# Attention with a feed-forward layer: one-bank PSUM tiles, 129-column products with v, and two jobs moved from VectorE to ScalarE

## The chip, the cores and the metric

The kernel runs on one core of a Trainium2 chip. Its time is the device time of one execution in microseconds (us); the median of several executions counts, and lower is better. Five engines work side by side: TensorE (PE in the profile; its weight loads are PEld), VectorE (DVE), ScalarE (ACT), GpSimd (POOL) and SyncE (SP), which issues the DMAs. Matrix products land in PSUM, which has eight banks of 512 float32 columns; all eight are in use here.

## The reference

```python
def _attn_ref(q, k, v):            # 8 batches, 8 heads, 1152 positions, 64 wide
    q_pool = q.reshape(B, H, S // 2, 2, D).mean(axis=3)
    scores = np.matmul(q_pool, k.transpose(0, 1, 3, 2)) / np.sqrt(D)
    scores = scores - np.max(scores, axis=-1, keepdims=True)
    attn = np.exp(scores)
    attn = attn / (np.sum(attn, axis=-1, keepdims=True) + 1e-09)
    return np.matmul(attn, v).astype(np.float32)

def _moe_ref(x, w_in, w_out):      # x: 4608 x 512, w_in: 512 x 2048, w_out: 2048 x 512
    h = x @ w_in
    g = h * np.cos(h)
    return (g @ w_out).astype(np.float32)

def reference(**kwargs):
    attn_out = _attn_ref(q, k, v)
    x = attn_out.transpose(0, 2, 1, 3).reshape(B * S, H * D)
    return _moe_ref(x, w_in, w_out)
```

## The kernel before, in words

The 64 heads are worked on two at a time: 32 pairs, each in ten units. Nine units of a pair hold the 128 keys of one block for both heads and 512 pooled queries each (2 x 512 score columns); one unit, the rest, holds the 64 remaining queries of each head against all nine key blocks (1024 and 128 columns). A unit runs as follows.

- `s_unit` writes the scores into a PSUM tile `st` of two banks (four products of 512 columns; a second product per bank subtracts the row maximum, which was folded into the operands beforehand). There is one such tile.
- `soft` (L1281 on) takes the exponential of all 1024 columns in one ScalarE instruction (L1299), casts the result to float16 (L1305), and forms the low half, the exponential minus its float16 copy: on GpSimd in two pieces of 512 columns (L1311), or, in every third unit from unit 80 on, on VectorE in one piece (L1307). `DSH` is that three.
- `av` (L1332 on) multiplies the 128 x 128 blocks of the exponential (loaded as weights) with v. v is 64 wide with a column of ones beside it, which gives the row sums. In float16 there are three products for each query tile of 128: high half with v's high half and the ones (65 columns), high half with v's low half (64 columns), low half with v's high half (65 columns). They add up in two PSUM banks, `ava` for the first head (and the rest) and `avb` for the second. For pairs 0 to 3, and for part of the key blocks of pairs 4 and 5, float32 products of 65 columns stand in their place (`NF32`).
- `av_end` (L1415 on) divides by the row sums on VectorE into `xp`.

The row maxima of a later pair come from products of their own, in PSUM tiles `mx` (printed as `m` or `mx`) of two banks, one tile at a time: `mx_main` (L788), `mx_rest` (L813), `mx_mixed` (L835), `mx_mixed_rest` (L851) and the `head_` and `first_` forms for the first three pairs. VectorE reduces 1024 columns at once (L811). Also ahead of a pair, q is pooled and cast twice over into `q1s` (`prep_q1`: one cast of 1024 columns and two of 64 x 128), on ScalarE for the first `QACT` = 6 pairs (L744) and on VectorE after (L746), and v's bound is taken (`v_max_begin`: the sum of squares on ScalarE for the first `VACT` = 6 pairs, L1115, the largest absolute value on VectorE after, L1119).

The feed-forward layer runs in 18 chunks of 256 tokens between the units: `ffn1` (L1586) into PSUM tiles `f` (two of one bank), two ScalarE passes and one VectorE pass out of them (L1610, L1613, L1614), a sine (L1518), a product on VectorE (L1524), a cast on ScalarE (L1535) and a subtraction on GpSimd (L1536), then `ffn2` (L1646). After the last pair only such chunks are left.

The order on each engine is written out by `arrange`. It takes all instructions in the order of the code, finds who needs whom (whole PSUM banks count), gives each a cost (`estimate`, with `HAND` for the hand-over between engines), and lays them out one after another: the next on an engine is the one that is ready by these costs and stands first in the code, moved by the `SHIFT` table. The engines then run their queues in that fixed order.

## Time and profile before

| | |
|---|---|
| median of 3 runs | 1517.22 us (1516.85 to 2447.02; the highest stands alone) |
| profiled execution | 1520.95 us, of which the trace spans 1519.2 us |
| PE busy | 1489.5 us (98%) |
| ACT busy | 1175.4 us (77%) |
| DVE busy | 1105.9 us (73%) |
| POOL busy | 922.4 us (61%) |
| mean granted clock of TensorE | 0.996 of full speed |

Busy time of an engine is the union of its instructions in the trace. Matmuls are pipelined, so the duration printed for one of them is longer than the time from its start to the next one's start; what a matmul takes of the engine is read from starts. A wait is idle time in front of an instruction, put down to whoever released it last.

### The profile page before, as it was taken

Reading aid. Unit: us, or ns where it says so; the run is one execution under the profiler, and the core shown is the slowest. Engines: PE = TensorE matmul, PEld = TensorE weight load, DVE = VectorE, ACT = ScalarE, POOL = GpSimd, SP = SyncE. Lnnn points to the kernel's source line nnn. Section 1 sums busy time; section 2 is a strip of 40 time slices with the busy share of each in tenths; the row PEclk is TensorE's granted clock in tenths of the full one; section 3 lists DMA queues with packets and bytes.
Section 4 is the critical chain, followed back from the end, with each engine's and each line's share of the span. In section 5 each row is a group of like instructions: output and inputs, shape, how many; then the busy total and the mean of one; then the engine's idle time right before and its main releaser. Section 6 shows DMA issues by size and latency. Waiting matters only on the chain.

```text
span 1519.2 us, 39331 instructions
## 1 busy us (share of the span) xinstructions
PE 1489.5 (98%) x16774; PEld 1027.7 (68%) x16774; DVE 1105.9 (73%) x1556; ACT 1175.4 (77%) x1475; POOL 922.4 (61%) x806
## 2 busy tenths in 40 slices
PE   6999999999999999999999999999999999999998
PEld 4777787657666576666667657666766667766665
DVE  7889987777878687887757877978788876442332
ACT  4867779888988789887967887997888888954442
POOL 4645757795775858577555576676766675430222
PEclk9999999999999999999999999999999999999999
DMA  9989543534255353435432335335344332001000
GB/s 268 246 237 188 151 109 69 107 82 119 73 108 97 89 110 80 110 91 114 85 75 64 80 74 125 76 91 126 82 104 99 73 63 32 10 27 30 20 16 22
DMA packets 226111, 145.15 MB, mean 96 GB/s; under 512 B 202448, under 2 KB 204752, under 8 KB 223888
## 3 DMA queue, kind: packets, MB, share of 16 engines
q1 hardware_dynamic: 225936, 142.65, 40.8%
q8 instruction: 131, 2.15, 0.6%
q14 instruction: 44, 0.36, 0.1%
HBM read 74.45 MB, written 10.49 MB: 56 GB/s over the span
## 4 chain that ended last, share of the span: by engine, by line
PE 89%; DVE 4%; DMA 3%; ACT 2%; issue 1%; SPq 0%; POOL 0%; ACTq 0%; DVEq 0%; POOLq 0%
PE f L1586 21%; PE f L1646 19%; PE st L1249 15%; PE ava L1325 8%; PE avb L1325 6%; PE m L797 6%; PE st L1272 2%; PE avb L1374 2%; PE mx L1646 1%; DMA wraw<-in_moe_w_in_dram 1%; PE mx L840 1%; PE st L1586 1%; PE mx L819 1%; DVE mxs L811 1%; DMA k<-kst 1%
## 5 line engine op out<-in xcount | busy, mean ns | idle before, releaser
L1311 POOL TENSOR_TENSOR pp<-e,pp 128x512 f16<-128x512 f32 x374 | 456.0, 1240 | 288.6 <-ACT pp L1305 151.3
L1586 PEld LDWEIGHTS <-w 128*128 128x128 f16 x3456 | 331.6, 98 | 61.5 <-issue 0.8
L1586 PE MATMUL f<-xT,w 128*128 128x256 f16 x3048 | 366.3, 273 | 0.0
L811 DVE TENSOR_REDUCE mxs<-m 128x2 f32<-128x1024 f32 x232 | 283.1, 1220 | 94.6 <-PE m L797 93.9
L1299 ACT ACTIVATE e<-st 128x1024 f32<-128x1024 f32 x267 | 272.5, 1021 | 96.5 <-PE st L1249 79.7
L1646 PE MATMUL f<-w,g 128*128 128x512 f16 x1440 | 333.7, 379 | 0.1
L1305 ACT CAST pp<-e 128x1024 f16<-128x1024 f32 x267 | 279.1, 1045 | 14.8 <-PE avb L1325 3.7
L1536 POOL TENSOR_TENSOR g<-hsc,g 128x512 f16<-128x512 f32 x144 | 192.1, 1354 | 157.7 <-ACT g L1535 150.3
L1325 PEld LDWEIGHTS <-pp 128*128 128x128 f16 (+1 forms) x7062 | 237.9, 100 | 65.5 <-issue 11.3
L1646 PEld LDWEIGHTS <-g 128*128 128x128 f16 x1680 | 158.5, 98 | 175.1 <-issue 0.7
L1249 PE MATMUL st<-q1T,k 128*128 128x512 f16 x576 | 219.3, 381 | 2.7 <-ACT pp L1299 1.9
L1249 PE MATMUL st<-q2T,k 128*128 128x512 f16 x576 | 219.2, 381 | 0.0
L1325 PE MATMUL ava<-vc,pp 128*128 128x65 f16 (+5 forms) x4502 | 218.2, 199 | 0.0
L1325 PE MATMUL avb<-vc,pp 128*128 128x65 f16 (+1 forms) x3052 | 179.0, 197 | 0.0
L1249 PEld LDWEIGHTS <-k 128*128 128x128 f16 x1152 | 104.5, 99 | 100.0 <-issue 11.0
L1524 DVE TENSOR_TENSOR hsc<-hsc,y 128x512 f32<-128x512 f32 x144 | 129.3, 933 | 37.8 <-ACT y L1518 37.5
L1614 DVE SCALAR_TENSOR_TENSOR y<-f,r1a,y 128x512 f32<-128x512 f32 x127 | 94.7, 746 | 66.6 <-ACT y L1613 64.1
L797 PE MATMUL m<-k,q1T 128*128 128x512 f16 x464 | 138.4, 380 | 4.2 <-ACT es L1299 1.7
L1307 DVE TENSOR_TENSOR pp<-e,pp 128x1024 f16<-128x1024 f32 x80 | 118.7, 1484 | 23.0 <-ACT pp L1305 22.7
L1610 ACT ACTIVATE hsc<-f,small 128x512 f32<-128x512 f32 x127 | 86.7, 682 | 58.4 <-PE f L1586 57.7
L1535 ACT CAST g<-hsc 128x512 f16<-128x512 f32 x144 | 83.4, 613 | 27.5 <-PE f L1646 26.2
L728 POOL TENSOR_TENSOR kst<-kld,kst 128x1152 f16<-128x1152 f32 x30 | 73.2, 2441 | 30.9 <-ACT kst L727 30.7
(189 smaller groups left out, 1852.0 us busy)
## 6 DMA issues: line engine op xcount, KB each, us to landing
vld<-in_v_dram SPq DMA_DIRECT2D x32, 576.0 KB, 4.5
kld<-in_k_dram SPq DMA_DIRECT2D x30, 576.0 KB, 4.2
qld<-in_q_dram SPq DMA_DIRECT2D x30, 576.0 KB, 4.4
k<-k SPq DMA_DIRECT2D x31, 288.0 KB, 3.7
wraw<-in_moe_w_in_dram SPq DMA_DIRECT2D x8, 1024.0 KB, 8.4
wraw<-in_moe_w_out_dram SPq DMA_DIRECT2D x8, 1024.0 KB, 6.1
out_dram<-ob SPq DMA_DIRECT2D x32, 256.0 KB, 2.5
left<-lx SPq DMA_DIRECT2D x64, 16.0 KB, 1.8
```

Of the source, the lines that this page charges most:

```text
L797: nc.tensor.matmul(banks[h], q1T[n][:, h * QT + t, :], kmain(n, k1[n % 3], c, h), start=True, stop=True, skip_group_check=True,),
L811: nc.vector.reduce_max(mxs[n][:, t : t + QT + 1 : QT, c], m, axis=AX.X)
L1249: nc.tensor.matmul(s[:, y, :].rearrange("p (t c) -> p t c", c=P), kcol(p, w, j, h), x[:, h * QT : (h + 1) * QT, :], start=part == 0, stop= ...
L1299: nc.scalar.activation(e, s, AF.Exp, scale=exp_scale, bias=l_add)
L1305: nc.scalar.copy(pp[:, 0, c0:n], e[:, c0:n])
L1307: nc.vector.tensor_sub(pp[:, 1, c0:n], e[:, c0:n], pp[:, 0, c0:n])
L1311: nc.gpsimd.tensor_sub(pp[:, 1, c], e[:, c], pp[:, 0, c])
L1325: mm = nc.tensor.matmul(out, w, x, start=start, stop=False, skip_group_check=True)
L1524: nc.vector.tensor_mul(hj, hj, y[:, j : j + 2])
L1536: nc.gpsimd.tensor_sub(gt[:, 1], hj, gt[:, 0])
L1586: mm = nc.tensor.matmul(ps[:, fi, :], w1[wt][:, hp, fs], ck.xT[hp][:, xi, cs], start=n == 0, stop=n == 3 * HP - 1, skip_group_check=True,)
L1646: nc.tensor.matmul(po, gt[:, gi, f % 2, ts_], w2[wt][:, f, :], start=f == 0 and (gi, wt) == (0, 0), stop=f == NF - 1 and (gi, wt) == (1, 0),)
```

## The change

- The PSUM tiles `st` and `mx` of two banks become one-bank tiles, two of each. A unit's scores stand in two tiles, and the exponential takes one instruction of 512 columns for each; the casts after it stay whole. The row maxima are reduced bank by bank. Tiles for the rests of the maxima take one bank where two were taken.
- In float16 units, three of four query tiles of the second head and two of four of the first take the high half's two products as one of 129 columns, written over v's low and high halves side by side. The two sums then lie 64 columns apart in PSUM (`COL`), and `av_end` adds them: it takes the row sums in two strided pieces for the first head, multiplies in two pieces, and adds the low part of each of the five tiles with one VectorE instruction (L1469 of the changed kernel).
- `QACT` and `VACT` go from 6 to 32: all casts of `q1s` and all bounds of v run on ScalarE.
- `DSH` goes from 3 to 5: from unit 80 on, every fifth low half is formed on VectorE instead of every third.
- `arrange` gets other costs: new constants in `estimate`, a hand-over of 0.203 us from PE, 0 from SP and 0.035 us from the others (0.21, 0.08 for ACT, 0.06 before), `INTO` added on the receiving engine, `OVER` subtracted where an instruction starts before the one ahead of it has ended, and a reader of a PSUM bank now waits for all writes to that bank. `SHIFT` holds the same numbers in another form.

```diff
-DSH = 3
+DSH = 5
...
-QACT = 6
+QACT = 32
...
-VACT = 6
+VACT = 32
...
-    "e": NE, "big": NBIG, "pp": NPP, "q1T": 3, "q2T": 2, "xp": NXP, "xT": NXT, "g": NG, "f": 2,
+    "e": NE, "big": NBIG, "pp": NPP, "q1T": 3, "q2T": 2, "xp": NXP, "xT": NXT, "g": NG, "f": 2, "mx": 2, "st": 2,
...
-HAND = {"PE": 0.21, "Activation": 0.08}
+HAND = {"PE": 0.203, "SP": 0.0}
+INTO = {"Pool": 0.07, "PE": 0.017}
+OVER = {"Activation": 0.094, "DVE": 0.083, "Pool": 0.042}
...
-                    if w:
-                        deps |= {j for j, bx in writes if hit(bx, bank)}
+                    deps |= {j for j, bx in writes if hit(bx, bank)}
...
     def mx_tile(n):
-        return psum.tile([P, 2, 512], F32, tag="mx", name="mx")
+        return [psum.tile([P, 512], F32, tag="mx", bufs=2, name="mx") for _ in range(2)]
...
-        if two:
-            for h in range(2):
-                nc.vector.reduce_max(mxs[n][:, h * QT + t, c : c + 1], banks[h], axis=AX.X)
-        else:
-            nc.vector.reduce_max(mxs[n][:, t : t + QT + 1 : QT, c], m, axis=AX.X)
+        for h in range(2):
+            nc.vector.reduce_max(mxs[n][:, h * QT + t, c : c + 1], banks[h], axis=AX.X)
...
-            s = psum.tile([P, 2, 512], F32, tag="st", name="st")
+            s = [psum.tile([P, 512], F32, tag="st", bufs=2, name="st") for _ in range(2)]
             for y, (h, j) in enumerate(banks_of(p, i)):
                 for w, x, part in ((ka, qa, 0), (kb, qb, 1)):
                     nc.tensor.matmul(
-                        s[:, y, :].rearrange("p (t c) -> p t c", c=P),
+                        s[y].rearrange("p (t c) -> p t c", c=P),
...
-            nc.scalar.activation(e, s, AF.Exp, scale=exp_scale, bias=l_add)
+            for a, b in enumerate(s):
+                c = slice(a * 512, min(a * 512 + 512, n))
+                nc.scalar.activation(
+                    e[:, c], b[:, 0 : c.stop - c.start], AF.Exp, scale=exp_scale, bias=l_add
+                )
...
+    WIDE = ((1, 2), (1, 2, 3))
+    STEP = 2 * D + 1
+    COL = ((0, STEP, 2 * STEP, 2 * STEP + D + 1), (0, STEP, 2 * STEP, 3 * STEP))
+    REST = 2 * STEP + 2 * (D + 1)
+    RUNS = (((0, 3, STEP), (3, 2, D + 1)), ((0, 4, STEP),))
...
+                    o = COL[h][t]
+                    wide = part == 0 and lo is not None and t in WIDE[h]
                     mm = av_mm(
-                        acc[h][:, t, :],
+                        acc[h][:, o - wide * D : o + D + 1],
                         w[:, c],
-                        vx[:, h, j] if lo is None else vn[:, h, j, D : 2 * D + 1],
+                        vx[:, h, j] if lo is None else vn[:, h, j, (1 - wide) * D : 2 * D + 1],
                         start,
                     )
...
                 for t in range(QT if part == 0 and lo is not None else 0):
-                    c = slice(h * 512 + t * P, h * 512 + (t + 1) * P)
-                    av_mm(acc[h][:, t, 0:D], w[:, c], vn[:, h, j, 0:D], False)
+                    if t not in WIDE[h]:
+                        c = slice(h * 512 + t * P, h * 512 + (t + 1) * P)
+                        o = COL[h][t]
+                        av_mm(acc[h][:, o : o + D], w[:, c], vn[:, h, j, 0:D], False)
...
-            nc.vector.tensor_scalar_add(rs[:, 0:n], acc[h][:, :, D], 1e-9 * PMAX)
+            for t0, m, step in RUNS[h]:
+                nc.vector.tensor_scalar_add(
+                    rs[:, t0 : t0 + m],
+                    strided(h, t0, m, step, D, 1).rearrange("p t d -> p (t d)"),
+                    1e-9 * PMAX,
+                )
...
+            for t in WIDE[h] if nf_of(p) < KT else ():
+                xt = xp[:, t, HALF[h]]
+                nc.vector.scalar_tensor_tensor(
+                    xt,
+                    acc[h][:, COL[h][t] - D : COL[h][t]],
+                    rs[:, t : t + 1],
+                    xt,
+                    ALU.mult,
+                    ALU.add,
+                )
```

On PE, inside the products with v of one float16 unit, the kernel before loads the same blocks of the exponential (`pp`) twice, once for 65 columns and once for 64; `vc_75` and `vc_76` are the two copies of v that alternate between pairs.

```order
L1325 MATMUL avb<-vc_75,pp 128x65
L1325 LDWEIGHTS pp
L1325 MATMUL avb<-vc_75,pp 128x65
L1325 LDWEIGHTS pp
L1325 MATMUL avb<-vc_75,pp 128x64
L1325 LDWEIGHTS pp
L1325 MATMUL avb<-vc_75,pp 128x64
```

The changed kernel has this on PE in the same place of a unit, for the first head.

```order
L1355 MATMUL ava<-vc_76,pp 128x65
L1355 LDWEIGHTS pp
L1355 MATMUL ava<-vc_76,pp 128x129
L1355 LDWEIGHTS pp
L1355 MATMUL ava<-vc_76,pp 128x129
L1355 LDWEIGHTS pp
L1355 MATMUL ava<-vc_76,pp 128x65
L1355 LDWEIGHTS pp
L1355 MATMUL ava<-vc_76,pp 128x64
```

Two of the first head's four tiles have one product with 129 columns where they had two; in the whole program the loads of `pp` as weights at this line go from 7062 to 5857, which is 1205 fewer, and the other counts on PE stay.

On ACT, at the end of the eighth pair (`rs`, the row sums' reciprocal for the rest, marks it), the kernel before runs exponentials (`e` from `st`), casts (`pp` from `e`) and the feed-forward layer's casts (`g` from `hsc`).

```order
L1299 ACTIVATE e<-st 128x1024
L1305 CAST pp<-e 128x1024
L1299 ACTIVATE es<-mx 128x128
L1305 CAST pps<-es 128x128
L1535 CAST g<-hsc 128x512 x3
L1299 ACTIVATE e<-st 128x1024
L1305 CAST pp<-e 128x1024
L1535 CAST g<-hsc 128x512
L1433 ACTIVATE rs<-rs,small 128x1
```

The changed kernel has this on ACT at the end of the same pair.

```order
L1580 CAST g<-hsc 128x512
L762 CAST q1s<-qld 128x1024
L1315 ACTIVATE e<-st 128x512 x2
L1580 CAST g<-hsc 128x512
L1323 CAST pp<-e 128x1024
L1478 ACTIVATE rs<-rs,small 128x1
L1131 ACTIVATE vc_76,mxa<-vld 128x18x64
L1580 CAST g<-hsc 128x512
L1315 ACTIVATE e<-st 128x512 x2
L762 CAST q1s<-qld 64x128
L1323 CAST pp<-e 128x1024
L762 CAST q1s<-qld 64x128
```

The exponential stands there in two pieces, and the casts of `q1s` and the bound of v (`mxa`) stand among the exponentials, where VectorE had them before.

On DVE, at the end of a pair, the kernel before frees `ava` and `avb` with these.

```order
L1425 TENSOR_SCALAR rs<-ava 128x5
L1426 RECIPROCAL rs<-rs 128x5
L1427 TENSOR_TENSOR xp<-ava,rs 128x4x64
L1425 TENSOR_SCALAR rs<-avb 128x4
L1426 RECIPROCAL rs<-rs 128x4
L1427 TENSOR_TENSOR xp<-avb,rs 128x4x64
```

The changed kernel has this on DVE in that place.

```order
L1454 TENSOR_SCALAR rs<-ava 128x3
L1454 TENSOR_SCALAR rs<-ava 128x2
L1454 TENSOR_SCALAR rs<-avb 128x4
L1459 RECIPROCAL rs<-rs 128x5
L826 TENSOR_REDUCE mxs<-m_6095 128x1
L1462 TENSOR_TENSOR xp<-ava,rs 128x3x64
L1459 RECIPROCAL rs<-rs 128x4
L1462 TENSOR_TENSOR xp<-ava,rs 128x64
L1469 SCALAR_TENSOR_TENSOR xp<-ava,rs,xp 128x64 x2
L1462 TENSOR_TENSOR xp<-avb,rs 128x4x64
L1485 TENSOR_SCALAR lx<-ava,rs 128x64
L1469 SCALAR_TENSOR_TENSOR xp<-avb,rs,xp 128x64
```

Four more instructions stand ahead of the last reader of `ava` (`lx`), and three more behind the product out of `avb`.

## Rows read from the trace of the kernel before

**Rows 1.** The page's first part: busy us (share of the span) and instructions.
```profile
PE 1489.5 (98%) x16774; PEld 1027.7 (68%) x16774; DVE 1105.9 (73%) x1556; ACT 1175.4 (77%) x1475; POOL 922.4 (61%) x806
```

**Rows 2.** Stretches: length, then busy us of PE, PEld, DVE, ACT, POOL, granted clock.
```profile
0.00:200.00 200.00, 178.93 (x1642) 136.45 (x1643) 172.36 (x263) 136.35 (x182) 111.12 (x134) 0.97 0.86 213
200.00:1300.00 1100.00, 1095.40 (x13532) 745.90 (x13530) 857.78 (x1186) 933.38 (x1146) 751.48 (x625) 1.00 0.40 89
1300.00:1500.00 200.00, 200.00 (x1488) 133.99 (x1487) 74.26 (x105) 105.68 (x148) 59.85 (x48) 1.00 0.06 20
550.00:600.00 50.00, 50.00 (x636) 34.76 (x634) 40.68 (x55) 47.76 (x59) 34.98 (x30) 1.00 0.37 81
950.00:1000.00 50.00, 50.00 (x647) 34.90 (x643) 43.66 (x57) 46.89 (x58) 34.81 (x30) 1.00 0.32 72
```

**Rows 3.** The chain of waits, 1200 to 1220 us: start us, us, what.
```profile
1201.19 0.86 PE st L1249 x4
1202.06 0.24 PE ava L1325 x8
1202.30 0.24 PE avb L1325 x8
1202.54 0.12 PE ava L1325 x4
```

**Rows 4.** Groups by form: `ava`'s 64-column products (`avb` has a row alike).
```profile
L1325 PE MATMUL ava<-vc,pp 128*128 128x64 f16 x964 | 67.9, 193 | 0.0
```

**Rows 5.** PE's instructions in order of time around 903 us: start us, us, what.
```profile
902.74 0.61 PE L819 MATMUL mx<-k,q1T 128*128 128x128 f16 x8
903.19 0.40 PE L1325 MATMUL ava<-vc,pp 128*128 128x65 f16 x8
```

**Rows 6.** Whom PE waited for: us in total, times, longest us.
```profile
PE m L955 <- DMA q1T<-q1s: 11.6, 1, 11.6
PE st L1249 <- ACT pp L1299: 1.9, 4, 0.8
...
PE mx L819 <- DVE mxs L849: 0.2, 1, 0.2
```

**Rows 7.** Groups of ACT by form: count, busy us, mean ns, idle before.
```profile
L1299 ACT ACTIVATE e<-st 128x1024 f32<-128x1024 f32 x267 | 272.5, 1021 | 96.5 <-PE st L1249 79.7 <-PE st L1272 6.3 <-POOL pp L1311 3.8
L1115 ACT ACTIVATE vc<-vld 128x1152 bf16<-128x1152 f32 x6 | 7.0, 1163 | 2.8 <-DMA vld<-in_v_dram 2.8
L1299 ACT ACTIVATE es<-mx 128x128 f32<-128x128 f32 x28 | 7.6, 271 | 4.0 <-PE mx L1272 3.9
L744 ACT CAST q1s<-qld 128x1024 f16<-128x1024 f32 x4 | 4.2, 1041 | 2.9 <-POOL qld L733 2.9
L744 ACT CAST q1s<-qld 64x128 f16<-64x128 f32 x8 | 2.3, 290 | 0.1
```

**Rows 8.** ACT's instructions in order of time around 901 us.
```profile
900.42 1.04 ACT L1305 CAST pp<-e 128x1024 f16<-128x1024 f32 x1
901.37 0.30 ACT L1632 ACTIVATE osc<-p2w,small 128x8 f32<-128x8 f32 x1
```

**Rows 9.** Groups of DVE and POOL by line and form.
```profile
L811 DVE TENSOR_REDUCE mxs<-m 128x2 f32<-128x1024 f32 x232 | 283.1, 1220 | 94.6 <-PE m L797 93.9
L899 DVE TENSOR_REDUCE mxs<-m 128x1 f32<-128x512 f32 x8 | 5.1, 681 | 0.8 <-PE m L884 0.8
L1307 DVE TENSOR_TENSOR pp<-e,pp 128x1024 f16<-128x1024 f32 x80 | 118.7, 1484 | 23.0 <-ACT pp L1305 22.7
L1119 DVE TENSOR_REDUCE mxa<-vld 128x1 bf16<-128x1152 f32 x26 | 35.0, 1346 | 4.4 <-DMA vld<-in_v_dram 4.3
L746 DVE CAST q1s<-qld 64x128 f16<-64x128 f32 x52 | 33.6, 647 | 0.7
L746 DVE CAST q1s<-qld 128x1024 f16<-128x1024 f32 x26 | 24.0, 923 | 0.2 <-POOL qld L733 0.2
L1440 DVE TENSOR_SCALAR lx<-ava,rs 128x64 f32<-128x64 f32 x32 | 8.9, 277 | 2.9 <-POOL pps L1311 1.6 <-ACT rs L1433 0.8 <-DMA xT<-xs 0.4
L1311 POOL TENSOR_TENSOR pp<-e,pp 128x512 f16<-128x512 f32 x374 | 456.0, 1240 | 288.6 <-ACT pp L1305 151.3 <-issue 107.5 <-POOL pp L1311 14.7
```

More of the change, by code (lines that the diff above doesn't have):

```diff
@@ L134, in estimate @@
     big = sum(a[2] > 1 for a in rd)
+    small = len(rd) - big
     if kind == "InstMemset":
@@ L139, in estimate @@
     if eng == "Pool":
-        return 0.16 + 0.00206 * n, True
+        wide = all(a[4] == 4 for a in rd + wr)
+        return 0.18 + 0.0019 * n + (0.13 if wide else 0.0), True
     if eng == "Activation":
-        return 0.145 + 0.00088 * n + 0.075 * (len(rd) - 1), False
+        c = 0.19 + 0.00083 * n + (0.1 if small else 0.0) - (0.025 if psum and n > 64 else 0.0)
+        return c + (0.19 if len(wr) > 1 else 0.0), False
     if kind == "InstTensorReduce":
-        return 0.1 + 0.00109 * n, False
+        return 0.155 + 0.00104 * n, False
     if kind == "InstTensorTensor" or (kind == "InstTensorScalarPtr" and big > 1):
-        return 0.15 + 0.00106 * n, not psum
+        return (0.21 if small else 0.15) + 0.00104 * n, not psum
     if kind == "InstTensorScalarPtr":
         if psum:
-            return 0.13 + 0.0012 * n, False
-        return 0.15 + 0.00055 * n, n > 1
-    return 0.13 + 0.00105 * n, False
+            return 0.2 + 0.00115 * n, False
+        return 0.15 + 0.00053 * n, n > 1
+    if kind == "InstTensorCopy" and not psum:
+        return 0.14 + 0.00053 * n, True
+    return 0.15 + 0.00104 * n, False
 def transfer(kind, src, dst):
@@ L272, in arrange @@
             nodes[a]["deps"].add(b)
+    for k in range(len(nodes) - 1):
+        if type(nodes[k]["ins"][0]).__name__ == "InstRegisterMove":
+            nodes[k + 1]["deps"].add(k)
     users = [[] for _ in nodes]
@@ L293, in arrange @@
             group += ("/".join(sorted(names))[:n],)
-        off += SHIFT.get(group, 0)
-        nd["key"] = (k + off + (len(nodes) if nd["ins"][0].name in fill else 0), k)
+        if nd["ins"][0].name in fill:
+            off += len(nodes)
+        elif group in SHIFT:
+            off += SHIFT[group][k * 1 // len(nodes)]
+        nd["key"] = (k + off, k)
     engines = ("PE", "Activation", "DVE", "Pool", "SP")
@@ L344, in arrange @@
             lock = end
-        now[e] = end
-        fin = end + HAND.get(e, 0.06)
+        now[e] = end - OVER.get(e, 0.0)
+        fin = end + HAND.get(e, 0.035)
         if e == "SP":
@@ L355, in arrange @@
         for j in users[k]:
-            r = done[k] if nodes[j]["eng"] != e or e == "SP" else end
+            if nodes[j]["eng"] != e:
+                r = done[k] + INTO.get(nodes[j]["eng"], 0.0)
+            elif e == "SP":
+                r = done[k]
+            else:
+                r = end + (0.033 if e != "PE" else 0.0)
             if (k, j) in issue:
@@ L792, in mx_main @@
         two = n < NMXF and mx_n[0] % 2
-        banks, m = first_tile(2, None if two else "mx")
+        banks, _ = first_tile(2, None if two else "mx")
         last = None
@@ L848, in mx_mixed @@
                 last = after(mm, last)
-        nc.vector.reduce_max(mxs[n][:, 2 * QT, 0:2], m, axis=AX.X)
+        for c in range(2):
+            nc.vector.reduce_max(mxs[n][:, 2 * QT, c : c + 1], m[c], axis=AX.X)
     def mx_mixed_rest(n):
@@ L944, in first_tile @@
         if main:
-            m = psum.tile([P, 2, 512], F32, tag=main, name="m0")
-            return [m[:, 0], m[:, 1]], m
+            return [psum.tile([P, 512], F32, tag=main, bufs=2, name="m0") for _ in range(two)], None
         return [psum.tile([P, 512], F32, tag="f", bufs=2, name="m0") for _ in range(two)], None
@@ L1262, in s_rem @@
         ka, kb, qa, qb = k1[p % 3], k2[p % 2], q1T[p], q2T[p]
-        if tag == "f":
-            s = psum.tile([P, 512], F32, tag=tag, bufs=2, name=tag).unsqueeze(1)
-        else:
-            s = psum.tile([P, 2, 512], F32, tag=tag, name=tag)
+        bank = lambda: psum.tile([P, 512], F32, tag=tag, bufs=2, name=tag)
+        s = [bank() for _ in range((j1 - j0 + RB - 1) // RB)]
         for j in range(j0, j1):
@@ L1336, in av @@
         if i == 0:
[L1337 to L1339 removed]
+            acc[0] = psum.tile([P, 512], F32, tag="ava", name="ava")
             order[0] = None
```

120 lines of the change are left out of this document (60 added, 60 removed).

## Prediction

> **What bounds the kernel now.** I began with the busy shares, went on to the stretches, and then read starts in the chain of waits. PE is busy 98% of the span and no other engine over 77% [rows 1]. By stretch, PE works 1095.40 of the 1100 us from 200 to 1300 us and all of the 200 us after, at the full granted clock [rows 2]. Only the first 200 us are loose: PE stands idle for 21 us there, with DVE at 172 of 200. A busy PE need not be a PE at its rate, since printed durations overlap; so the starts have to be looked at. In the chain, eight products with v take 0.24 us and the next eight start exactly as they end [rows 3], 30 ns apiece without a hole. PE's own work is therefore the bound over 1300 us. The time falls by what is taken off PE, by the 4.6 us of idle time in the middle, and by some of the 21 us at the start. It rises when another engine can no longer feed PE.
>
> **Merged products.** There are 964 products of 64 columns into `ava` and as many into `avb` [rows 4]. Two of four tiles of the first head and three of four of the second are merged, five eighths of 1928, which is the 1205 that the count of weight loads in the order shows. A merged pair took 2 x 30 = 60 ns [rows 3]. No row shows 129 columns; the nearest has 128, each with its own weight load: eight of them start at 902.74 and the next instruction at 903.19 [rows 5], so 0.45 / 8 = 56 ns, and 56.7 ns with the 129th column. That leaves 3.3 ns a pair, 1205 x 3.3 = 4.0 us, all of it on PE and so on the path. The ends are 0 (129 columns cost what the pair did) and 1205 x 4 = 4.8 us (the price of 128 columns). I take -4.0.
>
> Here a rule of the Trainium skill speaks against the change. "TensorE: Matmul & The Clock Gate", section "Back-to-back issue gap", gives about 81 ns for each 128-column matmul in a sustained stream of weight loads and matmuls. The trace disagrees: 56 ns [rows 5]. By that rule a merged pair would cost 21 ns more than before, not 3.3 less.
>
> **One-bank tiles on PE.** Behind the 11.6 us before the first product, PE's list of waits has 13 lines with 13.2 us in all, from 1.9 us for `st` down to 0.2 us [rows 6]; 12.3 us of them, 17 waits, are for ScalarE or VectorE to finish reading a tile of scores or maxima. With one-bank tiles, PE gets the first bank when half the read is done, and could run that bank's two matmuls there (four take 0.86 us [rows 3]), so each wait shrinks by 0.43 us at most: 17 x 0.43 = 7 us. The second bank comes free later than the whole did, by what the split costs (0.14 us for a reduction, below): 17 x 0.14 = 2 us the other way. New costs in the order shift these waits anyhow. I take -3 between -7 and +2.
>
> **More on ScalarE.** An exponential of 1024 columns takes 1021 ns and one of 128 takes 271 [rows 7], so a column costs 0.837 ns and 512 columns 592 ns. Two make 1184; but an independent instruction starts 0.09 us before the one ahead of it ends (901.37 against 900.42 + 1.04) [rows 8], so a unit pays 1184 - 90 - 1021 = 73 ns more, and 320 units 23 us. The moved casts of `q1s` are 26 pairs x (1041 + 2 x 290) ns = 42 us, the moved bounds of v 26 x 1163 = 30 us [rows 7]. ACT gets 95 us more, 1270 in all, and nearly all of it where it is fullest: from 200 to 1300 us 933 becomes about 1025 of 1100, 85% becomes 93%. What says that PE need not wait are the two densest stretches: ACT at 47.76 and 46.89 of 50 us (96 and 94%) and PE at 50.00 in both [rows 2]. What is queued behind a moved cast are exponentials and the passes that empty `f`; PE waits for both, and has the other kind of work (feed-forward matmuls while an exponential is late, products while `f` is) to cover about one microsecond. The bounds of v also bring a wait for v's DMA to ACT's queue: 2.8 us in six now, so up to 12 us over 26 [rows 7]. I charge +3 for covers that run short, with 0 below; the upper end is a rival's.
>
> **Less on VectorE, more on GpSimd.** Off VectorE go 24.0 + 33.6 us of casts, 35.0 us of bounds, and 32 of 80 low halves of 1484 ns, 47 us. On it come the split reductions, 2 x 681 - 1220 = 142 ns each and 33 us for the 232 of L811, and at the end of a float16 pair (28 of them have merged tiles) seven small instructions; the nearest row is a 64-column one out of PSUM at 277 ns, so 28 x 7 x 0.277 = 54 us [rows 9]. VectorE ends some 50 us lighter. On the path is one thing: `ava` is read for 4 x 0.277 = 1.1 us longer before the next pair may write it. Scores and feed-forward matmuls stand there for PE, and no line of PE's waits names that end now; I cost it at nothing. Without the cover it would be 28 x 1.1 = 31 us, and a sixth of that, 5 us, goes into the range. GpSimd takes 64 more pieces of 1240 ns, 79 us [rows 9], and goes from 751 to about 830 of 1100 us: the units concerned get their low half 2 x 1.24 - 1.48 = 1 us later, with the same cover.
>
> **The start.** In the first 200 us the casts and bounds were on ScalarE already, so DVE, the fullest engine there, only gains split reductions: six pairs of some eight, 48 x 0.142 = 7 us if all of it showed. Against it, a reduction can begin one product earlier, and reductions of different banks overlap as ACT's instructions do. I take 0, between -4 and +7.
>
> **The sum** is -4.0 - 3 + 3 + 0 = -4 us on the profiled execution's 1520.95, or 1517. The median of the runs lies 3.7 us below that execution, so the forecast for a median is **1513 us**. Its ends, not all at once, are 1503 and 1522.
>
> **Rivals.**
> - *ScalarE becomes the bound (slower).* The exponentials, casts and passes in its queue need 1025 us of the 1100. This decides as soon as ACT cannot run denser than 93% over that length, whatever it does for 50 us. At 92% the stretch takes 1114 us, at 90% 1139: 14 to 39 us more, less the 7 from PE, so 1524 to 1549; I put it at 1535. For it: 85% now with gaps between exponentials that wait for scores (96.5 us before L1299 [rows 7]). Against it: those gaps are ACT waiting for PE, and the densest stretches. 10%.
> - *Nothing gained.* The 129 columns cost what the pair did and the waits for tiles move elsewhere: 0 + 0 + 3, so 1517 to 1520. The change then does its work, but PE's share of it is empty. For it: the gain of 3.3 ns a pair is the difference of two readings of 0.01 us. 20%.
> - *The waits go.* PE gets all 7 us of the tiles and half of the idle 21 us at the start, since no read holds two banks and the order is made with other costs: -4.8 - 7 - 10, so 1495 to 1500. 12%.
> - *A merged product is bound by its weight load and the stream around it,* as wide products would be if the gap between them were set by more than their columns. The mechanism would have to add some 20 ns to each of 1205, +25 us: 1538. Against it: the 56 ns of rows 5, where each product also has its own load. 3%. (It is the time that the page's 81 ns would give.)
>
> **How the numbers follow.** The forecast keeps 55%. The range from 1501 to 1527 holds the forecast's cases, the empty gain, the better part of the cases below 1503 and the mild end of ScalarE's; it leaves out some 15%. A measurement of this kernel can tell about 2% from no change, which is 1487 below and 1548 above. Nothing in the cases reaches 1487 but a start without idle time and more, 2%; over 1548 lies the dense end of ScalarE's rival with a cover lost beside it, 5%; 93% is within.
>
> **What the changed profile would show.** Right: L1355's 129-column products in the chain at 56 to 57 ns apiece, PE busy over 99% from 200 to 1300 us, ACT there at some 93%, exponentials of about 592 ns, DVE lighter by some 50 us, and no wait of PE over 1 us for `st` or `mx` after the start. Wrong: PE waiting for `e`, `pp` or `f`'s readers on ACT in that stretch for more than 10 us, starts of the merged products 60 ns or more apart, or a start where PE first multiplies scores several us later. The forecast fails if ACT's fixed order leaves PE without work near the pairs that have both casts and weights, or if the new costs lay out the first 200 us differently by more than the 7 us allowed.

## The result, and the profile after

The changed kernel takes 1530.1 us (median of 12 runs, 1521.0 to 1535.6) against 1517.1 us: 1.0075 times as long, 95% interval 1.0054 to 1.0095. That is 13 us, less than 2% but plainly more than nothing; 1513 was forecast, in a range that ended at 1527. Its runs fall into two groups, five from 1521.0 to 1525.5 and seven from 1528.9 to 1535.6, where those of the kernel before lie within 4 us but for one that stands alone. The profiled execution, 1523.91 us with a span of 1522.1, is of the lower group. A second series of the same kernel, called `again` below, was profiled in the upper one: 1531.1 us, span 1529.3.

Busy times of the changed kernel, and its stretches (columns as in [rows 1, 2]):

```profile
PE 1489.3 (98%) x15569; PEld 1022.5 (67%) x15569; DVE 1042.9 (69%) x1935; ACT 1231.5 (81%) x1925; POOL 978.7 (64%) x852
```

```profile
0.00:200.00 200.00, 176.71 (x1606) 132.53 (x1607) 173.21 (x325) 138.15 (x233) 106.91 (x115) 0.99 0.82 214
200.00:1300.00 1100.00, 1094.39 (x12366) 742.05 (x12366) 792.61 (x1495) 986.18 (x1538) 809.47 (x687) 1.00 0.40 89
1300.00:1500.00 200.00, 200.00 (x1474) 135.20 (x1472) 75.57 (x112) 107.19 (x156) 60.22 (x49) 1.00 0.07 21
```

Between 200 and 1300 us ACT went from 933 to 986 us, POOL from 751 to 809, DVE from 858 down to 793 [rows 2], and PE is as busy as before: in this execution no engine looks overrun. The groups that the change touched, by form:

```profile
L1315 ACT ACTIVATE e<-st 128x512 f32<-128x512 f32 x534 | 295.8, 604 | 48.6 <-PE st L1265 26.7 <-POOL pp L1329 13.3 <-PE st L1286 3.8
L826 DVE TENSOR_REDUCE mxs<-m 128x1 f32<-128x512 f32 x464 | 304.0, 681 | 109.9 <-PE m L815 108.1
L1325 DVE TENSOR_TENSOR pp<-e,pp 128x1024 f16<-128x1024 f32 x48 | 84.8, 1767 | 31.1 <-ACT pp L1323 22.8 <-PE m L815 4.5 <-POOL pp L1329 1.5
L1329 POOL TENSOR_TENSOR pp<-e,pp 128x512 f16<-128x512 f32 x438 | 531.0, 1236 | 235.7 <-ACT pp L1323 121.2 <-issue 71.7 <-PE avb L1355 9.7
L1355 PE MATMUL avb<-vc,pp 128*128 128x129 f16 x723 | 80.5, 220 | 0.0
L1355 PE MATMUL ava<-vc,pp 128*128 128x129 f16 x482 | 67.0, 220 | 0.0
```

The 1205 merged products are there, 723 + 482. The low halves left on VectorE now last 1767 ns each, not 1484 [rows 9], the first sign that VectorE and GpSimd get in each other's way. In the chain of waits of the changed kernel (start us, us, what), PE's own work comes out as costed:

```profile
1208.31 0.23 PE ava L1355 x6
1208.55 0.23 PE avb L1355 x5
```

Six products (two of 129 columns, two of 65, two of 64) or five (three of 129, one of 65, one of 64) take 0.23 us where eight took 0.24 [rows 3]; from 1208.31 to the next start at 1208.77 are 0.46 us for what were 0.48.

Where the time went is read from PE's starts. For each matmul I took the time to the next one's start, less the time that this form takes back to back in these traces (29 and 30 ns for 64 and 65 columns, 56 for 129, 216 for 512, half of it in 64 columns of the array). What is left is lost, by waiting or at the half clock. Here is what PE lost in each stretch, in us, with the time of matmuls at their own rate ahead of it, and how long the records show TensorE at 1.2 GHz. `n3`, below, is the kernel before with one number of its order's table changed; its profiled execution, the quickest of its eleven, stands for the kernel before, whose own (1520.95 us) is 4 us over its median. All versions are told in the next section.

```
kernel (profiled, us)  own rate  0-50  50-200  200-350  350-1300  at 1.2 GHz
n3            1516.87   1467.2    7.3     5.8      2.5      16.5         0.0
before        1520.95   1467.2    7.7     9.3      2.2      16.8        10.2
after         1523.91   1464.2    7.5    11.7      2.3      20.0         3.4
again         1531.10   1464.2    6.6    11.7     11.6      18.8        10.2
p_gate        1527.93   1464.2    7.0    11.7      9.0      17.9        10.2
u_dsh         1521.26   1464.2    6.9    11.7      2.2      17.5         0.0
u_move        1524.48  1464.2    6.9    16.6      3.1      15.4        13.7
u_wide        1522.84  1467.2    7.1    11.6      3.3      16.1         3.4
core3         1526.23   1467.2    7.1    14.6      3.0      16.8        13.7
b_dsh         1525.00   1467.2    8.4     4.4      2.3      22.3         3.4
s_early       1520.78   1464.2    7.1     9.2      4.3      17.1         3.4
s_early_move  1523.94   1464.2    7.2     9.2      5.4      20.1         6.8
n4            1534.94   1464.2    7.1    14.5      9.9      20.9        13.7
u_bank        1531.55   1464.2    8.0    21.5      2.8      16.4        23.9
u_cost        1536.00   1464.2    7.3     9.8     13.5      23.3         6.8
a_bank        1532.25   1467.2    6.6     8.8     11.4      19.9         6.8
a_cost        1539.49   1467.2    7.5    24.2      4.8      17.8        20.5
```

Against `n3`, `again` is 14.2 us longer: -3.0 for the products, -0.7 in the first 50 us, +5.9 between 50 and 200, +9.1 between 200 and 350, +2.3 up to 1300 and +0.5 behind. `again`, a run of the upper group, differs from `after`, one of the lower, in one stretch, 200 to 350 us. This is VectorE, and then GpSimd, in `again` at 336 us:

```profile
335.31 0.68 DVE L866 TENSOR_REDUCE mxs<-mx 128x1 f32<-128x512 f32 x1
335.91 8.23 DVE L1525 SCALAR_TENSOR_TENSOR xs<-xp,ratio,xs 128x512 f16<-128x512 f32 x1
344.07 0.68 DVE L845 TENSOR_REDUCE mxs<-mx 128x4 f32<-128x512 f32 x1
```

```profile
334.55 1.17 POOL L1581 TENSOR_TENSOR g<-hsc,g 128x512 f16<-128x512 f32 x1
335.66 2.28 POOL L1329 TENSOR_TENSOR pp<-e,pp 128x512 f16<-128x512 f32 x2
337.90 1.15 POOL L1581 TENSOR_TENSOR g<-hsc,g 128x512 f16<-128x512 f32 x1
339.01 2.26 POOL L1329 TENSOR_TENSOR pp<-e,pp 128x512 f16<-128x512 f32 x2
341.23 2.36 POOL L746 TENSOR_TENSOR kst<-kld,kst 128x1152 f16<-128x1152 f32 x1
```

One VectorE instruction that reads two SBUF tiles, the split of x (it makes the low half of the feed-forward layer's input from `xp` and the high half), lasts 8.23 us: it begins under the first of six GpSimd pieces without a gap and ends 0.55 us after the last (341.23 + 2.36). Behind it stand the reductions of row maxima, and PE waits for them. Its clock falls to 1.2 GHz during the wait, at 340.4 us, and stays there for 10.2 us, 5.9 us beyond the wait's end; over these 20 us it stands at 0.76 of full speed on average (time, then busy us of PE, PEld, DVE, ACT, POOL, granted clock):

```profile
344.80 0.37 PE L873 MATMUL mx<-k,q1T 128*128 128x128 f16 x2 [6.71 <-DVE mxs L845]
```

```profile
330.00:350.00 20.00, 13.29 (x142) 7.37 (x140) 14.86 (x21) 11.73 (x20) 13.59 (x12) 0.76 0.41 65
```

In the profiled execution of the lower group the same instruction starts 0.26 us after the same GpSimd piece, as in `again` (0.25), and lasts 1.47 us. It got in between two pieces, GpSimd's second piece waited (2.75 us for two, not 2.28), and PE was busy for all 20 us:

```profile
336.88 2.75 POOL L1329 TENSOR_TENSOR pp<-e,pp 128x512 f16<-128x512 f32 x2
```

```profile
337.14 1.47 DVE L1525 SCALAR_TENSOR_TENSOR xs<-xp,ratio,xs 128x512 f16<-128x512 f32 x1
```

```profile
330.00:350.00 20.00, 20.00 (x216) 11.13 (x215) 16.21 (x31) 17.29 (x29) 18.43 (x16) 1.00 0.50 100
```

That VectorE's two-input reads and GpSimd exclude each other is in the Trainium skill, "SBUF — State Buffer", section "Who interferes with whom": such an instruction "contends with a GpSimd instruction that reads SBUF", and the first gets the port pair for a whole instruction. The traces agree for one instruction; that the loser can miss every handover of a run of six is what `again` shows beyond it. It is the exception: in the profiled execution of the lower group 26 of the 32 splits of 512 columns begin under a GpSimd piece and take 1.13 us in the median and 1.88 at most, and the six that do not take 0.75. The traces also show that two inputs are not needed. In the kernel before, the 23 casts of 128 columns from SBUF (`q1s`, one input) that begin outside a GpSimd piece take 224 ns in the median and the 29 that begin under one 1090, while reductions of 1024 columns out of PSUM (L811) take 1219 and 1225 ns.

### The profile page after: what moved, and what is told of

The parts are those of the page before. It is cut to its first block, busy times and chain, and to the rows that moved or that the text cites. A ratio compares the mean times of both kernels' runs of the same rounds, so it can differ in the third digit from the quotient of the medians.

```text
span 1522.1 us, 37816 instructions
## 1 busy us (share of the span) xinstructions
PE 1489.3 (98%) x15569; PEld 1022.5 (67%) x15569; DVE 1042.9 (69%) x1935; ACT 1231.5 (81%) x1925; POOL 978.7 (64%) x852
## 4 chain that ended last, share of the span: by engine, by line
PE 84%; DVE 6%; ACT 5%; DMA 2%; issue 1%; POOL 1%; SPq 0%; ACTq 0%; DVEq 0%; POOLq 0%
PE f L1630 20%; PE f L1690 19%; PE st L1265 14%; PE ava L1355 8%; PE avb L1355 6%; PE m L815 6%; PE st L1286 2%; DVE mxs L826 2%; PE mx L1690 1%; DMA kld<-in_k_dram 1%; ACT e L1315 1%; PE ava L1400 1%; ACT pp L1323 1%; PE st L1630 1%; PE mx L856 1%
## 5 line engine op out<-in xcount | busy, mean ns | idle before, releaser
L1329 POOL TENSOR_TENSOR pp<-e,pp 128x512 f16<-128x512 f32 x438 | 531.0, 1236 | 235.7 <-ACT pp L1323 121.2
L826 DVE TENSOR_REDUCE mxs<-m 128x1 f32<-128x512 f32 x464 | 304.0, 681 | 109.9 <-PE m L815 108.1
L1315 ACT ACTIVATE e<-st 128x512 f32<-128x512 f32 x534 | 295.8, 604 | 48.6 <-PE st L1265 26.7
L1581 POOL TENSOR_TENSOR g<-hsc,g 128x512 f16<-128x512 f32 x144 | 185.9, 1312 | 172.3 <-ACT g L1580 136.9
L1355 PE MATMUL ava<-vc,pp 128*128 128x65 f16 (+6 forms) x4020 | 214.6, 202 | 2.3 <-DVE lx L1485 1.5
L1355 PE MATMUL avb<-vc,pp 128*128 128x65 f16 (+3 forms) x2329 | 176.8, 207 | 0.3 <-POOL pp L1329 0.3
L1569 DVE TENSOR_TENSOR hsc<-hsc,y 128x512 f32<-128x512 f32 x144 | 133.8, 962 | 40.4 <-ACT y L1563 40.1
L815 PE MATMUL m<-k,q1T 128*128 128x512 f16 x464 | 154.6, 380 | 4.8 <-DVE mxs L826 4.1
L1580 ACT CAST g<-hsc 128x512 f16<-128x512 f32 x144 | 88.7, 626 | 30.6 <-PE f L1690 29.6
L1325 DVE TENSOR_TENSOR pp<-e,pp 128x1024 f16<-128x1024 f32 x48 | 84.8, 1767 | 31.1 <-ACT pp L1323 22.8
```

Source lines behind the costliest of these rows:

```text
L815: nc.tensor.matmul(banks[h], q1T[n][:, h * QT + t, :], kmain(n, k1[n % 3], c, h), start=True, stop=True, skip_group_check=True,),
L826: nc.vector.reduce_max(mxs[n][:, h * QT + t, c : c + 1], banks[h], axis=AX.X)
L1315: nc.scalar.activation(e[:, c], b[:, 0 : c.stop - c.start], AF.Exp, scale=exp_scale, bias=l_add)
L1329: nc.gpsimd.tensor_sub(pp[:, 1, c], e[:, c], pp[:, 0, c])
L1355: mm = nc.tensor.matmul(out, w, x, start=start, stop=False, skip_group_check=True)
L1569: nc.vector.tensor_mul(hj, hj, y[:, j : j + 2])
```

## The experiments

Each time is a median, the ratio is to the kernel before measured beside it (1517.3 to 1518.3 us).

### One part undone in the changed kernel

**u_move**, casts and bounds back on VectorE.

```diff
-QACT = 32
+QACT = 6
-VACT = 32
+VACT = 6
```

> The changed kernel with the casts of q1s and the bounds of v back on VectorE after pair 6 (QACT = VACT = 6), all else as changed. Theory A (ScalarE too full: with 986 of 1100 us busy, any lateness of it reaches TensorE): the time falls by 8 to 15 us to 1515 to 1522 and the spread of runs from 15 us to under 5. Theory B (the new costs of the order leave it without slack, so lateness on any engine reaches TensorE): within 4 us of the changed kernel's 1530, spread as wide. Theory C (one-bank tiles, with their split exponentials and reductions, cost it): 1526 to 1531.

Measured: 1522.96 us (1519.4 to 1525.7), 1.0030 [1.0017, 1.0043].

**u_cost**, the old costs, hand-over times and table in `arrange` (`HAND = {"PE": 0.21, "Activation": 0.08}`, no `INTO` or `OVER`).

> The changed kernel with the order laid out by the costs of the kernel before (estimate, hand-over, dependencies), all else as changed. Theory B: 1512 to 1519 and a spread under 5 us. Theory A: no better than 1526, spread as wide. Theory C: no better than 1526.

Measured: 1536.00 us (1532.9 to 1542.4), 1.0125 [1.0103, 1.0147]. In this kernel the new costs are not what loses: without them it is 6 us slower.

**u_bank**, the tiles of two banks again, one exponential and one reduction each.

```diff
-        return [psum.tile([P, 512], F32, tag="mx", bufs=2, name="mx") for _ in range(2)]
+        return psum.tile([P, 2, 512], F32, tag="mx", name="mx")
...
```

> The changed kernel with two-bank tiles for scores and maxima again, one of each, one exponential per unit and whole reductions; all else as changed. Theory C: 1513 to 1520 with a small spread. Theory A: 4 to 6 us below 1530, since ACT loses 23 of its 95 us. Theory B: 1527 to 1533.

Measured: 1531.55 us (1526.7 to 1533.7), 1.0083 [1.0068, 1.0099]. No change, but for another reason: its trace has no split of x over 3 us, and 21.5 us lost between 50 and 200 us, where the changed kernel loses 11.7.

**u_wide**, products of 65 and 64 columns again.

```diff
-    WIDE = ((1, 2), (1, 2, 3))
+    WIDE = ((), ())
```

> The changed kernel with no merged products (all products with v of 65 and 64 columns again, no additions in av_end), all else as changed. By the prediction's price of 3.3 ns a pair: 4 us slower than the changed kernel, 1534. If the merge gains nothing: 1530. If the additions at the end of a pair are what costs (ava held longer): 1522 to 1527. Theories A, B and C all expect the first.

Measured: 1522.91 us (1521.1 to 1526.1), 1.0034 [1.0024, 1.0044]. Quicker by 7 us, though PE has 3.0 us more to do (1467.2 against 1464.2): what its new order avoids is the loss at 336 us. It has all of GpSimd's extra pieces, and the split begins there inside a run of them too, but gets in at the end of the piece under way, and GpSimd's next two take 2.73 us for 2.28:

```profile
337.35 0.88 DVE L1525 SCALAR_TENSOR_TENSOR xs<-xp,ratio,xs 128x512 f16<-128x512 f32 x1
```

```profile
337.63 2.73 POOL L1329 TENSOR_TENSOR pp<-e,pp 128x512 f16<-128x512 f32 x2
```

In `u_move`, again with all the pieces, it takes 1.06 us, and no run of either version is over 1526.2 us.

### One part done alone in the kernel before

**a_bank**, one-bank tiles alone (the diff of `u_bank` the other way round).

> The kernel before with the one-bank tiles alone (split exponentials and reductions with them), all else as before. Theory S (the loss lies in the first 200 us, where VectorE is the fullest engine and split reductions make it later; TensorE idles there and its granted clock halves for a few us): 1521 to 1528, mean clock under 1.000 in most runs, idle time of TensorE in the first 200 us 4 us or more above before's. Theory A (ScalarE too full from 200 to 1300 us): 1517 to 1519, since ACT gains only 23 us. If one-bank tiles do what the prediction gave them: 1514.

Measured: 1535.13 us, 1.0112 [1.0098, 1.0126].

**a_cost**, the new costs alone.

> The kernel before with the order laid out by the new costs alone. If the new costs leave the start without slack: 1522 to 1532, clock under 1.000. If they only make the order truer (as the run with the old costs, 1536, says for the changed kernel): 1511 to 1517, clock 1.000.

Measured: 1538.05 us, 1.0137 [1.0123, 1.0150].

**a_wide**, the merged products alone (`WIDE` and `COL` as in the change).

> The kernel before with the merged products and the additions in av_end alone. By the prediction's price: 1513, and the 129-column products start 56 to 58 ns apart. If the longer hold of ava at the end of a pair costs more than the merge gives (theory W, after the run without the merge was 7 us faster than the changed kernel): 1519 to 1525, with TensorE waiting for VectorE's lx, rs or xp at the ends of pairs.

Measured: 1531.46 us, 1.0087 [1.0073, 1.0101].

**a_move**, casts and bounds on ScalarE alone (`QACT = 32`, `VACT = 32`).

> The kernel before with the casts of q1s and the bounds of v of all pairs on ScalarE alone (QACT = VACT = 32). Theory A: 1520 to 1528, the loss of TensorE between 250 and 1300 us and ACT above 91% there. If ScalarE has the room that the prediction gave it: 1515 to 1519. Theory S says the same as the latter, as the first six pairs do not change.

Measured: 1525.19 us, 1.0054 [1.0042, 1.0067].

All four lose, 59 us together where the whole change loses 13. The parts do not add up, since each makes `arrange` write another order. So I asked what a new order costs by itself.

### What another order costs

**n2**, **n3**: the kernel before with one number of `arrange` changed. **n4**: the changed kernel likewise. **again**: the changed kernel once more.

```diff
-HAND = {"PE": 0.21, "Activation": 0.08}
+HAND = {"PE": 0.215, "Activation": 0.08}
```
```diff
-    ("DVE", "TensorRe", "wmx", "big"): -20,
+    ("DVE", "TensorRe", "wmx", "big"): 0,
```
```diff
-HAND = {"PE": 0.203, "SP": 0.0}
+HAND = {"PE": 0.208, "SP": 0.0}
```

> The kernel before with one number of the order changed (the hand-over from PE 0.215 us in place of 0.21): the same instructions, 2521 of 32140 places on PE's queue differ. Theory P (the order before is an unusually good one among orders of the same work, and whatever re-lays it loses): 1520 to 1530, with idle time of TensorE in the first 350 us and clock under 1.000. Theory Q (each part of the change costs what its run alone showed, 8 to 20 us, by its own work): 1515 to 1519.

> The kernel before with another number of the order changed (the SHIFT of the weights' maxima on VectorE 0 in place of -20): the same instructions, 1726 places on PE's queue differ. Theory P: 1520 to 1530. Theory Q: 1515 to 1519.

> The changed kernel with one number of the order changed (the hand-over from PE 0.208 us in place of 0.203): the same instructions. Theory P: anywhere from 1518 to 1538, more than 3 us from the changed kernel's 1530. Theory Q: 1527 to 1533.

> The changed kernel once more, for a second trace of it: 1521 to 1536. If the execution is one of the slower, its extra time should lie in the first 350 us (theory S) as idle time and half clock of TensorE; if ScalarE's fullness spreads the runs (theory A), in waits between 350 and 1300 us.

Measured: n2 1520.47 us, 1.0019 [1.0011, 1.0028]; n3 1518.19, 1.0008 [0.9999, 1.0016]; n4 1531.97 (1523.1 to 1534.9), 1.0073 [1.0052, 1.0094]; again 1531.19 (1527.4 to 1535.5), 1.0092 [1.0079, 1.0105]. A small shift of the order costs 1 to 3 us (n2, n3 and n4 have 9, 6 and 1% of PE's matmuls in another place). The versions with a part undone or done alone have 31 to 55% in another place where it can be counted, and `a_cost` shows what that alone can cost: it has the matrix, vector and scalar work of the kernel before in another order (44% of the matmuls, and two more table loads on ScalarE) and is 20 us slower. So the time of a version prices none of its parts, and a large new order alone could cost the 13 us; a cause has to be read from a place in a trace. n4's trace has the held split too, 8.23 us and 6.7 of waiting, in an execution of 1534.94 us.

### GpSimd's pieces

**p_gate** keeps all of the change and its order (3% of PE's matmuls stand in another place), and lets GpSimd copy one element of the low half of x after each split of x, so that its next piece waits for the split. The rest of the edit, not shown, tells `arrange` to lay the copies out without moving anything else. (There are 40 splits, 32 of 512 columns and 8 of 256; the 28 in the expectation is a miscount.)

```diff
             xs2[:, 1, :nt], xp[:, :nt], ratio, xs2[:, 0, :nt], ALU.mult, ALU.subtract
         )
+        seen = sb2.tile([P, 1], F16, tag="seen", bufs=1, name="seen")
+        nc.gpsimd.tensor_copy(seen, xs2[:, 1, 0, 0:1])
```

> The changed kernel, in which GpSimd copies one element of the low half of x after each of the 28 splits of x, so that its next piece cannot start before VectorE has finished that split; the rest of the order stays nearly as it was. Held theory: the slow half of the changed kernel's runs (1527 to 1536 us; the others lie at 1521 to 1525.5) comes from one VectorE split of x that GpSimd's pieces, run back to back, hold for 8.2 us at 336 us; with the pause no such split lasts over 4 us, no wait of PE after 200 us is over 3 us, and all runs lie at 1519 to 1526. Clock theory (the half clock in the first 350 us falls by itself and makes the spread): runs still spread from 1521 to 1536 with a median of 1528 to 1532. A pause that costs GpSimd more than it gives would show as 1528 to 1535 without a held split.

Measured: 1528.07 us (1522.9 to 1530.4), 1.0063 [1.0051, 1.0076]. As numbers, the held theory's were missed; the trace says why. The copy stands only behind the fifth piece of the run in GpSimd's queue. VectorE, GpSimd and PE of `p_gate`:

```profile
336.23 5.93 DVE L1538 SCALAR_TENSOR_TENSOR xs<-xp,ratio,xs 128x512 f16<-128x512 f32 x1
```

```profile
339.33 2.28 POOL L1342 TENSOR_TENSOR pp<-e,pp 128x512 f16<-128x512 f32 x2
342.22 0.19 POOL L1542 COPY seen<-xs 128x1 f16<-128x1 f16 x1 [0.61 <-DVE xs L1538]
342.36 2.36 POOL L759 TENSOR_TENSOR kst<-kld,kst 128x1152 f16<-128x1152 f32 x1
```

```profile
342.81 0.37 PE L886 MATMUL mx<-k,q1T 128*128 128x128 f16 x2 [4.41 <-DVE mxs L858]
```

GpSimd stops after its fifth piece, not the sixth (`kst`, 2.36 us). The split again ends 0.55 us after GpSimd's last piece and lasts 5.93 us in place of 8.23, PE waits 4.41 in place of 6.71: each 2.3 us less, the length of the piece that now comes after. Once the split is held, the length of GpSimd's run sets the length of the hold.

**u_dsh**: the changed kernel with `DSH = 3`, every third low half on VectorE. **b_dsh**: the kernel before with `DSH = 5`, and nothing else. **core3**: the changed kernel with `DSH = 3`, `QACT = VACT = 6` and `WIDE = ((), ())`, so that one-bank tiles and the new costs are left.

> The changed kernel with every third low half on VectorE again and not every fifth: GpSimd some 75 us lighter between 200 and 1300 us, VectorE 45 us heavier. Held theory: fewer pieces back to back, no split of x held over 4 us, median 1519 to 1525. Theory that ScalarE's 53 us more are the loss: no change, 1527 to 1532. Theory that VectorE's load is what counts: slower, 1532 to 1537.

> The kernel before with every fifth low half on VectorE instead of every third, and nothing else: GpSimd some 75 us busier. Held theory: 1520 to 1530, with a VectorE instruction that reads two SBUF tiles held over 3 us and a wait of PE behind it. Prediction's view (GpSimd's pieces lie under the same cover): 1515 to 1519. If only a new order counts: 1518 to 1522 without such an instruction.

> The changed kernel with only its one-bank tiles and its order's new costs kept: the merged products, the casts and bounds on ScalarE and the fewer low halves on VectorE all taken back. If the loss comes from what ScalarE and GpSimd were given: 1515 to 1519, as the kernel before. If one-bank tiles under the new costs lose by themselves (split reductions, more VectorE instructions): 1521 to 1527. If any order but the old one loses: 1520 to 1530.

Measured: u_dsh 1521.17 us (1520.1 to 1525.0, 11 runs), 1.0025 [1.0017, 1.0034]; b_dsh 1524.64 (1523.6 to 1525.6), 1.0045 [1.0033, 1.0057]; core3 1523.58 (1522.0 to 1526.5), 1.0040 [1.0027, 1.0053].

Taking the 64 extra pieces from GpSimd gives back 9 us (8 by the ratios) and ends the upper group of runs, though VectorE has 26 us more to do from 200 to 1300 us (818.27 against 792.61). In `u_dsh` GpSimd and then VectorE at the same place read:

```profile
335.30 2.72 POOL L1329 TENSOR_TENSOR pp<-e,pp 128x512 f16<-128x512 f32 x2
337.98 1.16 POOL L1581 TENSOR_TENSOR g<-hsc,g 128x512 f16<-128x512 f32 x1
339.09 3.36 POOL L746 TENSOR_TENSOR kst<-kld,kst 128x1152 f16<-128x1152 f32 x1
```

```profile
336.20 0.80 DVE L1525 SCALAR_TENSOR_TENSOR xs<-xp,ratio,xs 128x512 f16<-128x512 f32 x1
338.79 1.43 DVE L1325 TENSOR_TENSOR pp<-e,pp 128x1024 f16<-128x1024 f32 x1
```

The two pieces that GpSimd had at 339 us are VectorE's one low half here, and now `kst` is the one that waits a microsecond (3.36 for 2.36).

In the kernel before, the same move costs 7 us, with no single long hold: the longest loss after 200 us is at 699 us, where three casts of q1, 2.2 us by the means of [rows 9], take 3.10 and a split of x of 256 columns, 0.48 in the median of the changed kernel, takes 1.28, beside four GpSimd pieces in a row. PE then stands 2.07 us and runs 3.4 us at 1.2 GHz, some 4 us in all (an estimate: the wait and half of the 3.4). VectorE, GpSimd and PE of `b_dsh`:

```profile
696.43 3.10 DVE L746 CAST q1s<-qld 128x1024 f16<-128x1024 f32 x3
699.56 1.28 DVE L1480 SCALAR_TENSOR_TENSOR xs<-xpl,ratio,xs 128x256 f16<-128x256 f32 x1
```

```profile
695.60 4.95 POOL L1311 TENSOR_TENSOR pp<-e,pp 128x512 f16<-128x512 f32 x4
```

```profile
701.62 1.77 PE L1586 MATMUL f<-xT,w 128*128 128x256 f16 x12 [2.07 <-DVE ratio L1470]
```

core3 loses 6 us with neither GpSimd's pieces nor ScalarE's work: one-bank tiles and the new costs together are no gain. But the new costs with two-bank tiles lose 20 (`a_cost`), so under these costs the tiles give some 14 back.

### The start, and ScalarE's work

**s_early**: `u_dsh`, whose order is laid out with the old costs while its own clock is under 200 us. **s_early_move**: the same with `QACT = VACT = 6`.

```diff
+        early = t0 < EARLY
...
+        c = nd.get("cost0", nd["cost"]) if early else nd["cost"]
```

> The changed kernel with every third low half on VectorE, whose order is laid out with the old costs and hand-over times in its first 200 us and with the new ones after. Start theory (what is left of the loss, 3.4 us, is made between 50 and 200 us, where the traces of all kernels with the new costs stand 11 to 22 us against PE's own rate and those with the old ones mostly 4 to 10): 1515 to 1518, with 5 to 9 us against PE's rate there. If the new costs are harmless in the start and the tiles of one bank are what costs there: 1520 to 1523, with 11 us or more.

> The same with the casts of q1 and the bounds of v on VectorE again after the sixth pair, so that one-bank tiles, merged products and the late new costs are left. If ScalarE's 53 us cost PE the 4 us that stood between the pairs of kernels with and without the move between 350 and 1300 us: 2 to 5 us less than the kernel beside it, 1511 to 1515. If that loss was only the accident of an order: within 1.5 us of it. If VectorE's extra load counts: 3 us more or worse.

Measured: s_early 1520.37 us (1519.2 to 1524.0), 1.0020 [1.0011, 1.0029]; s_early_move 1524.93 (1523.2 to 1530.5), 1.0055 [1.0041, 1.0069]. The old costs take 2.5 us of the loss from 50 to 200 us (9.2, not 11.7), and most of that comes back behind it (4.3, not 2.2, from 200 to 350); the time fits the second theory, the loss neither. Taking the casts off ScalarE again costs 4.6 us, where in the changed kernel it gave 7. ScalarE's load is therefore not what loses by itself; the two versions with the fullest ScalarE, `u_dsh` with ACT at 995 us of the 1100 and `s_early` at 993, are the quickest of the changed versions. No version beat the kernel before.

## Why the prediction was wrong

**GpSimd: the step that failed.** "GpSimd takes 64 more pieces ... with the same cover" was costed at nothing. The 64 pieces are there (438 against 374) and their results come in time; the cover was the wrong question. Each piece also shuts out VectorE's reads of two SBUF tiles and its casts from SBUF. In `again` one such hold of 8.23 us makes PE wait 6.71, and 9.1 us more than in `n3` are lost from 200 to 350 us; the sign that the prediction named for being right, no wait of PE over 1 us for `st` or `mx`, fails there. In times, taking the pieces back gives 9 us in the changed kernel (`u_dsh`), and adding them alone costs 7 (`b_dsh`), but these are no price of the pieces: `u_move` and `u_wide` keep them all and lose the upper group too. The pieces make GpSimd's run at that place longer by two (`u_dsh` has VectorE's low half there); whether a split with PE's work behind it is caught in one hangs on the order and, as `after` and `again` show, on the execution. For the changed kernel the mechanism is shown by `p_gate`, which shortens the hold and PE's wait by the length of one piece, and by the held split in each of the three traces above 1527 us of the changed kernel and its near copies (`again`, `n4`, `p_gate`) and its absence at 1523.9. For untraced runs of the upper group it is inferred. In `b_dsh` it is read from one place worth some 4 us of the 7. A sign stood in [rows 9]: a cast of 128 columns out of SBUF took VectorE 647 ns on average, nearly as long as a reduction of 512 columns out of PSUM (681), and I did not ask why; 29 of these 52 began under a GpSimd piece.

**Merged products: right.** -4.0 was forecast. By the closest starts of each form PE's own time fell by 3.0 (a pair was 59 ns, not 60); from start to start (gaps over 0.12 us left out) the float16 products with v over 128 rows take 174.0 us in the kernel before and in `u_wide` and 170.5 in the changed kernel, 3.5 less. No total shows it, since every comparison has another order. The rival of a product bound by its weight load is refuted by 0.23 us for six. (Its 1538 took the 25 us from 1513, a sum that already held the gain of 4; counted from before it is 1542.)

**One-bank tiles: the -3 did not show, and they have no fixed sign.** -3 between -7 and +2 was forecast. Done alone, under the old costs, they lose 18 us (`a_bank`); under the new costs alone they give some 14 back (`a_cost` to `core3`); in the changed kernel undoing them changes nothing. Single waits of PE for `st`, `m` and `mx` did shrink: in the profiled execution none is over 0.5 us after 200 us, where the kernel before has three, up to 1.4. What the waits gave is less than what the order does elsewhere, above all before 200 us.

**The start: at the edge of its range.** 0 between -4 and +7 was forecast; against `n3` 5.9 us more were lost from 50 to 200 us, the same 11.7 in `after`, `again`, `p_gate` and `u_dsh`. Against the kernel before's own trace, which loses 9.3 there, it is 2.4, so some of it may be the spread of executions. The rest points at the new costs' order, and not at one-bank tiles: with the new costs and two-bank tiles 21.5 (`u_bank`) and 24.2 us (`a_cost`) are lost there, with the new costs and one-bank tiles 11.6 to 16.6, and with one-bank tiles laid out by the old costs 8.8 to 9.8 (`a_bank`, `s_early`, `u_cost`), about as much as in the kernel before's own trace. Each is one execution; which instruction of the new order is late was not followed, so this stays open.

**ScalarE: mis-sized, and not a cost.** 95 us more were forecast, 56 came (1175.4 to 1231.5). The lengths of its instructions in the trace add up to 151 us more (1245.7 to 1396.4), but they overlap by 165 us in place of 70; of these 95 us of overlap the prediction had counted 29, for the exponentials alone. The stretch from 200 to 1300 us is 89.7% full, not 93%. The charge of +3 has no fixed price: undoing the move gives 7 us in one order and costs 4.6 in another, and a move alone costs 8 (`a_move`). The rival that ScalarE becomes the bound did not come about.

**VectorE** got 63 us lighter, where 50 was forecast, at no visible gain: `u_dsh` gives it 26 us back from 200 to 1300 us and is quicker. What the held split shows to count is when it may read.

**`ava` held longer**, costed at nothing: PE's list of waits after names one such wait, 1.5 us at 171 us, and `u_wide`, which has no merged products, has the same one. No cost of the longer hold shows.

## What to carry to other kernels

Before moving work from VectorE to GpSimd, list what VectorE reads from two SBUF tiles or casts from SBUF beside it, and what is queued behind those reads: the worst case seen here is the length of GpSimd's unbroken run, not of one piece, and the busy share of the two engines (69 and 64% here) does not tell it. In a kernel whose order is laid out by a list of costs, one edit is many: perturb the order alone first, a little and by much (here 1 to 3 us and 20), and take no part's price from times alone. An engine that is 98% busy can still lose 9 us to one wait, here 6.7 us standing still and the rest at the half clock behind it; compare a quick and a slow execution of the same kernel before comparing two kernels.

## What was not expected of the hardware

Two executions of the same order, with the same VectorE instruction starting 0.25 or 0.26 us into the same GpSimd piece, differ by 6.8 us in its length (8.23 against 1.47). In `again`, `n4` and `p_gate` it misses the first handover and then all until GpSimd's run ends: 8.23 us behind six pieces, twice, and 5.93 behind five. What decides the first handover is not known. A cast from one SBUF tile is held as well (224 ns or 1090), a reduction out of PSUM is not (1219 or 1225). PE's 6.71 us of waiting were followed by a granted clock of 0.76 over the 20 us around them, where the quick execution has 1.00.
